# Level 6 of a chunked RWKV-6 attention in quarters of the TensorE array, its masked copies replaced by rectangles

## The chip, the cores and the metric

One core of one Trainium2 chip. The metric is the device time of a whole launch in microseconds (us), lower is better. The kernel before takes 628.2 us, the median of three runs (627.67 to 628.48).

## What is computed

An RWKV-6 attention with a decay for each channel (4 batch rows, 8 heads, 768 steps, head size 48), and behind it a feed-forward block with a SiLU (3072 tokens, 384 to 2048 to 384), all in float32:

```python
for t in range(S):
    cur = np.einsum('bhd,bhe->bhde', u[None] * kt, vt)
    y[:, :, t] = np.einsum('bhd,bhde->bhe', rt, state + cur)
    state = wt[:, :, :, None] * state + np.einsum('bhd,bhe->bhde', kt, vt)
...
x = np.ascontiguousarray(attn_out.transpose(0, 2, 1, 3)).reshape(B * S, H * D)
h = x @ w_in
g = h * (1.0 / (1.0 + np.exp(-h)))
return (g @ w_out).astype(np.float32)
```

## The kernel before, in words

**Units.** The work is cut into 12 units, numbered from 0: 6 chunks of 128 time steps, each for 2 batch rows (b = 0 and 1). In a unit the 8 heads of a batch row are 4 pairs p with two heads e = 0 and 1 each; head e of a pair lies on partitions 64e to 64e + 47 of the transposed tokens. The tokens of batch row 1 are kept in reversed order in places, so that one product serves both rows.

**Levels.** Inside a chunk the recurrence is unrolled by doubling. The scores of a step against an earlier one are found at the level l at which the two fall into the two halves of a block of 2c steps, c = 2^l; levels run from 0 to 6, and at level 6 (c = 64) there is one block: the queries of steps 64 to 127 against the keys of steps 0 to 63. `tr` holds the queries, `tk` the keys and `tw` the products of decays; from level to level, queries (`grow_queries` L604, `prepare` L729) and keys (`grow_keys` L610, `odd_keys` L592) are multiplied by those products.

**Score products.** `score_products` (L661) makes a level's scores with 8 matmuls, one for each pair p and head e. Each takes 48 rows of keys, 128 key columns wide, and moves 128 query columns, 64 of each batch row; the two heads lie on the two row halves of the array and write two PSUM tiles, `sc[0]` and `sc[1]`. So every level computes 128 by 64 scores for each head and batch row, of which the mask of the level keeps a part. `keep_masked` (L676) copies the kept part into the tile `score` with one predicated copy on VectorE (DVE) for each e. For level 6 the mask keeps a plain rectangle for each batch row: 64 rows by 64 columns. `scores` (L682) does products and copies one after the other, and already uses rectangles on ScalarE (ACT) at L698 for the copies listed in COPIED, all of unit 0.

**Bursts.** From unit 2 on (NTOK = 2) levels 3 and 4, and 5 and 6, are made in bursts (`burst`, L743): both levels' products stand one behind the other on TensorE (PE), level 5 in the tile p_sc and level 6 in p_m (in unit 2 in p_o). The copies of a burst follow in `keep_level` (L751), the growing of keys and queries in `go_on` (L755).

**After the scores.** The bonus term (the u of the reference) is written over `score` on its diagonal: in units 2 and 3 by `bonus_spread` (L561, the ACT copies L575 and L577, the DVE shuffle L578) and `bonus_write` (L581, the predicated copies L584), later by `block_spread` and `block_write` (L546 and L553, L557), ahead of the burst of levels 5 and 6. Unit 2 is the one unit from there on whose bonus comes behind that burst. `turn_k` (L773) transposes the keys on PE, which ACT copies to kq (L782). `y_state` (L789, L794) multiplies the state with the queries, `y` (L797, L807) the scores with the values, and `update` (L813, L821) makes the new state; GpSimd (POOL) decays the state at L826, DVE adds to it at L835. `move_x` moves the outcome by DMA to xt.

**Feed-forward.** `up` (L924, L929) multiplies xt with w_in and ACT applies the SiLU from PSUM (L938; two PSUM buffers, p_h). From unit 1 on the second product is done by `quarter` (L981, L995), seven products for eight in the manner of Strassen, whose sums of gt DVE makes at L977; before that `down` (L946, L951).

**Order.** Every engine works through its own queue in the order in which the program was written out, with waits on semaphores; nothing is reordered by a planner. The order is written by hand: units 0 to 2 in a list of `do` calls (L1036 to L1093), the others in `mix` (L867), which gives groups of attention steps, between which L1095 to L1107 put `up` and `quarter` steps of earlier units. In unit 2 the line is

```python
do((burst, 2, 5), (keep_level, 2, 5), (keep_level, 2, 6), (go_on, 2, 6), (up, 1, 6), (bonus_spread, 2), (bonus_write, 2),
   (load_values, 3), *both(turn_k, 2), (up, 1, 7), (sums, 1, 2))
```

and in later units the burst, `keep_level` 5 and 6 and `go_on` 6 are one group, followed by `up` steps.

Of the kernel before, what the change touches and what calls it, by code (L numbers as in the profile page):

```python
# [38 lines left out]
def kernel(  # L39
# [11 lines left out]
    nc = tc.nc  # L51

    B, H, S, D = r.shape
    DM, DF = moe_w_in.shape
    L = 128
    NL = 7
    NB = 2
    NP = H // 2
    PD = 64
    Q = NB * NP  # L60
    NX = Q + 2 * NP
    X = 0, NP + Q
# [5 lines left out]
    NTOK = 2  # L68
# [250 lines left out]
    NSC = 1  # L319
    score = const.tile([128, NSC, 2, Q, L], F32, name="score")  # L320

    masks = {}
    first = {}
    for l in range(NL):
        c, ni = 1 << l, L >> (l + 1)
# [18 lines left out]
    tw, tr, tk, diag, kq, xt = {}, {}, {}, {}, {}, {}  # L344
# [311 lines left out]
        start_keys(i, nc.gpsimd, False)  # L656


    COPIED = (0, 5, 0), (0, 6, 0), (1, 6, 0)

    def score_products(i, l, queries, sc):  # L661
        c, ni = 1 << l, L >> (l + 1)

        for p in range(NP):
            for e in range(2):
                rows = slice(PD * e, PD * e + D)

                apart, r_p, s_p = 2 * (NP - p) - 1, queries[rows, p, :], sc[e][:, p, :]
                nc.tensor.matmul(bass.AP(tensor=s_p.tensor, offset=s_p.offset,  # L669
                                         ap=[s_p.ap[0], [apart * L // 2, 2], [1, L // 2]]),  # L670
                                 lhsT=tk[i][rows, X[l % 2] + p, :],
                                 rhs=bass.AP(tensor=r_p.tensor, offset=r_p.offset + c,
                                             ap=[r_p.ap[0], [apart * L, 2], [2 * c, ni], [1, c]]),
                                 start=True, stop=True)

    def keep_masked(i, l, e, sc):  # L676
        c, ni = 1 << l, L >> (l + 1)
        dst = score[:, i % NSC, e].rearrange("p (b q) (i s c) -> p b q i s c", b=NB, s=2, c=c)[:, :, :, :, 1, :]
        nc.vector.copy_predicated(out=dst, mask=masks[l][:, :, None].to_broadcast([128, NB, NP, ni, c]),  # L679
                                  data=sc[e].rearrange("p (b q) (i c) -> p b q i c", b=NB, c=c))  # L680

    def scores(i, l, *between):  # L682
        c, ni = 1 << l, L >> (l + 1)

        name = "p_h" if i == 0 and l % 2 == 1 else "p_sc"
        sc = [ps.tile([128, Q, L // 2], F32, name=name, bufs=2) for e in range(2)]
        score_products(i, l, tr[i], sc)
        if i < NTOK and l + 2 < NL:
            odd_keys(i, l + 1)

        def keep(e):
            if (i, l, e) in COPIED:

                for b in range(NB):
                    for x in range(ni):
                        first = 2 * x * c if b == 0 else L - (2 * x + 1) * c
                        rows, columns = slice(first, first + c), slice((2 * x + 1) * c, (2 * x + 2) * c)
                        nc.scalar.copy(out=score[rows, i % NSC, e, b * NP:(b + 1) * NP, columns],  # L698
                                       in_=sc[e][rows, b * NP:(b + 1) * NP, x * c:(x + 1) * c])
                return  # L700
            keep_masked(i, l, e, sc)
# [39 lines left out]
    made = {}  # L741

    def burst(i, l):  # L743

        other = (second[0], "p_o") if i == NTOK else (ps, "p_m")
        for x, (pool, name) in enumerate(((ps, "p_sc"), other)):
            made[i, l + x] = [pool.tile([128, Q, L // 2], F32, name=name, bufs=2) for e in range(2)]
        score_products(i, l, before.pop((i, l)), made[i, l])
        score_products(i, l + 1, tr[i], made[i, l + 1])

    def keep_level(i, l):  # L751
        for e in range(2):
            keep_masked(i, l, e, made[i, l])

    def go_on(i, l):  # L755

# [110 lines left out]
    def mix(i):  # L867
# [22 lines left out]
        if i < NPAIR:  # L890
            groups = [[*both(turn, i, "w"), (product, i, 0)],
                      [*both(turn, i, "k"), *both(turn, i, "r"), (odd_ones, i)], [(start_levels, i), (prepare_keys, i, 1)],
                      [(prepare, i, 1), *[(product, i, l) for l in range(1, NL)]],
                      [(burst, i, 1), (keep_level, i, 1)],
                      [(keep_level, i, 2), (go_on, i, 2)],
                      [(prepare, i, 3), (reverse_v, i), (bonus, i, 0)],
                      [(burst, i, 3), (keep_level, i, 3), (bonus_sum, i, 0), (bonus, i, 1), (bonus, i, 2)],
                      [(keep_level, i, 4), (go_on, i, 4), (bonus_sum, i, 1), (load_rk, i + 1), (load_u,)],
                      [(prepare, i, 5), (make_block_mask,), (bonus_spread, i), (bonus_write, i)],
                      [(burst, i, 5), (keep_level, i, 5), (keep_level, i, 6), (go_on, i, 6)], *end]  # L900
        else:
            groups = [[], [(odd_keys, i, 2), (grow_keys, i, 2, False), (grow_queries, i, 2), *sum_steps(i, 2)],
                      [(prepare, i, 3), *bonus_steps(i, 6, 7)],
                      [(burst, i, 3), (keep_level, i, 3), *sum_steps(i, 3, 4), (block_move, i), *at(ahead, (load_rk, i + 1))],
                      [(keep_level, i, 4), (go_on, i, 4)],
                      [(prepare, i, 5), (reverse_v, i)],
                      [(block_spread, i), (block_write, i)],
                      [(burst, i, 5), (keep_level, i, 5), (keep_level, i, 6), (go_on, i, 6)], *end]
# [231 lines left out]
```

## Time and profile before

| | |
|---|---|
| median of 3 runs | 628.2 us (627.67 to 628.48) |
| the profiled execution's own time | 628.39 us |
| its span | 626.6 us |
| PE busy | 620.3 us (99%) |
| DVE busy | 438.6 us (70%) |
| POOL busy | 363.7 us (58%) |
| ACT busy | 187.4 us (30%) |
| granted TensorE clock | 1.00 |

The profile is one execution of the program. Times are in us from the start of its span, unless marked ns. A line of a group or of the timeline names the kernel's line, the engine, the operation, the tile written and the tiles read, the shapes, and how many instructions are taken together. PE is the matmul and PEld the load of its weights, which overlaps other matmuls; every float32 matmul of the program leaves two records of each. The length of a matmul record is longer than the distance to the next one, since matmuls are pipelined: what a matmul costs is read from start to start. The chain of work is followed back from the last instruction to what released each step.

### The profile page before, as it was taken

The page shows a single profiled execution, that of the slowest core. Times are in us where ns is not written, and L with a number is a line of the kernel's source. Part 1 is how long each engine was busy: PE and PEld are TensorE (multiplying, and loading weights), DVE is VectorE, ACT ScalarE, POOL GpSimd, SP SyncE. Part 2 cuts the span into 40 slices and gives each one's busy share as a digit, 9 for nine tenths or more (in the row PEclk, how much of TensorE's full clock was granted, in tenths as well). Part 3 has the DMA queues.
Part 4 walks back from the last instruction along what each step waited for, and adds up shares of the span by engine and source line. Part 5 has one row for each costly group of instructions (what it writes and reads, how often), then busy time and mean ns, then how long its engine had stood idle before and what let it go on. Part 6 is the DMA issues. An engine that isn't in the chain of part 4 may idle for free.

```text
span 626.6 us, 12324 instructions
## 1 busy us (share of the span) xinstructions
PE 620.3 (99%) x4606; PEld 562.8 (90%) x4606; DVE 438.6 (70%) x749; ACT 187.4 (30%) x380; POOL 363.7 (58%) x414
## 2 busy tenths in 40 slices
PE   8999999999999999999999999999999999999997
PEld 8888876799899899899899899889889989989997
DVE  6879779898995694794794595686596596571041
ACT  6798882221321320320320321221221221220110
POOL 6998388566676567567577378378378458400000
PEclk9999999999999999999999999999999999999999
DMA  9966874443543643543543543542542312100000
GB/s 227 291 154 163 164 203 49 88 79 66 101 68 50 133 66 68 106 69 63 105 67 54 110 65 52 115 64 51 115 70 50 77 33 51 35 1 27 25 1 25
DMA packets 203067, 53.25 MB, mean 85 GB/s; under 512 B 186752, under 2 KB 194816, under 8 KB 203008
## 3 DMA queue, kind: packets, MB, share of 16 engines
q1 hardware_dynamic: 201424, 51.88, 41.1%
q10 hardware_dynamic: 1584, 0.59, 0.4%
q8 instruction: 36, 0.59, 0.4%
q14 instruction: 23, 0.19, 0.1%
HBM read 43.21 MB, written 5.24 MB: 77 GB/s over the span
## 4 chain that ended last, share of the span: by engine, by line
PE 94%; POOL 1%; DVE 1%; ACT 1%; DMA 1%; issue 1%; POOLq 0%; ACTq 0%
PE p_h L929 41%; PE p_o L995 32%; PE p_sc L669 5%; PE p_m L951 3%; PE p_m L807 3%; PE p_m L794 3%; PE p_m L669 3%; PE p_m L781 1%; PE p_sc L821 1%; DMA raw<-in_k_dram 1%; PE p_m L372 1%; POOL tk L625 1%; PE p_m L845 0%; DVE score L584 0%; POOL w_in_sb L241 0%
## 5 line engine op out<-in xcount | busy, mean ns | idle before, releaser
L929 PE MATMUL p_h<-xt,w_in_sb 128*128 128x256 f32 x1152 | 258.1, 382 | 0.7 <-POOL tk L649 0.7
L929 PEld LDWEIGHTS p_h<-xt,w_in_sb 128*128 128x128 f32 x1152 | 215.9, 190 | 32.6 <-POOL tk L649 0.9
L938 ACT ACTIVATE gt<-p_h 128x512 f32<-128x512 f32 x90 | 53.7, 597 | 256.1 <-PE p_h L929 255.9
L625 POOL TENSOR_TENSOR tk<-tk,tw 128x256 f32<-128x256 f32 x128 | 88.7, 714 | 62.4 <-ACT tk L595 34.7
L995 PE MATMUL p_o<-own,temps 128*128 128x192 f32 x528 | 87.9, 326 | 0.0
L995 PE MATMUL p_o<-w_out_sb,gt 128*128 128x192 f32 x508 | 87.3, 328 | 0.0
L995 PEld LDWEIGHTS p_o<-own,temps 128*128 128x128 f32 x528 | 86.0, 190 | 0.2
L995 PEld LDWEIGHTS p_o<-w_out_sb,gt 128*128 128x128 f32 x508 | 82.7, 190 | 0.9 <-issue 0.4
L487 POOL TENSOR_TENSOR ruk<-tokens_rk 128x768 f32<-128x768 f32 (+1 forms) x32 | 48.5, 1527 | 46.3 <-DMA tokens_rk<-in_k_dram 33.7
L977 DVE TENSOR_TENSOR temps<-gt 128x256 f32<-128x256 f32 x84 | 55.4, 660 | 18.3 <-ACT gt L938 18.3
L408 POOL TENSOR_TENSOR tw<-tw 128x256 f32<-128x256 f32 (+6 forms) x83 | 43.8, 528 | 40.2 <-DVE tw L360 36.3
L679 DVE COPY_PREDICATED score<-mask,p_sc 128x512 f32<-128x512 int8 x62 | 44.5, 772 | 13.4 <-PE p_sc L669 12.7
L607 DVE TENSOR_TENSOR tr<-tr,tw 128x512 f32<-128x512 f32 x61 | 49.6, 813 | 3.7 <-POOL tk L625 1.1
L595 ACT COPY tk<-tk 128x256 f32<-128x256 f32 x52 | 20.9, 403 | 85.4 <-POOL tk L625 67.1
L1004 DVE TENSOR_TENSOR partial<-p_o,partial 128x192 f32<-128x192 f32 x33 | 11.8, 358 | 47.2 <-PE p_o L995 47.1
L669 PEld LDWEIGHTS p_sc<-tr,tk 48*128 48x128 f32 x512 | 31.4, 187 | 10.3 <-issue 7.3
L669 PE MATMUL p_sc<-tr,tk 48*128 48x128 f32 x512 | 37.7, 285 | 0.7 <-POOL tk L625 0.6
L1004 DVE TENSOR_TENSOR temps<-p_o,partial 128x192 f32<-128x192 f32 x22 | 7.9, 358 | 33.3 <-PE p_o L995 23.1
L995 PE MATMUL p_o<-w_out_sb,temps 128*128 128x192 f32 x176 | 30.4, 326 | 0.0
L995 PEld LDWEIGHTS p_o<-w_out_sb,temps 128*128 128x128 f32 x176 | 28.9, 190 | 0.0
L487 POOL TENSOR_TENSOR tokens_rk<-tokens_rk,tokens_w 128x192 f32<-128x192 f32 (+1 forms) x32 | 26.8, 857 | 1.3
L977 DVE TENSOR_TENSOR temps<-temps,gt 128x256 f32<-128x256 f32 x43 | 25.7, 598 | 1.5
(170 smaller groups left out, 828.0 us busy)
## 6 DMA issues: line engine op xcount, KB each, us to landing
w_out_sb<-in_moe_w_in_dram SPq DMA_DIRECT2D x6, 768.0 KB, 7.0
w_out_sb<-in_moe_w_out_dram SPq DMA_DIRECT2D x4, 768.0 KB, 5.1
own<-in_moe_w_out_dram SPq DMA_DIRECT2D x4, 768.0 KB, 5.1
tokens_rk<-in_r_dram SPq DMA_DIRECT2D x8, 384.0 KB, 4.5
tokens_rk<-in_k_dram SPq DMA_DIRECT2D x8, 384.0 KB, 5.3
tokens_w<-in_w_dram SPq DMA_DIRECT2D x8, 384.0 KB, 6.6
xt<-yt SPq DMA_DIRECT2D x60, 48.0 KB, 2.0
raw<-in_w_dram SPq DMA_DIRECT2D x80, 32.0 KB, 2.3
```

What stands on the lines that cost most here:

```text
L408: engine.tensor_tensor(out=up, in0=t[:, :, 0::2], in1=t[:, :, 1::2], op=ALU.mult)
L487: mul = lambda out, one, two: nc.gpsimd.tensor_tensor(out=out, in0=one, in1=two, op=ALU.mult)
L595: nc.scalar.copy(out=keys(i, X[(l + 1) % 2] * L + c, [4 * c, blocks], [c, 2], [1, c]), in_=keys(i, NP * L + c, [4 * c, blocks], [NP * L + ...
L607: nc.vector.tensor_tensor(out=odd, in0=odd, in1=tw[i][l][:, :, 0::2][:, :, :, None].to_broadcast([128, Q, L >> (l + 1), c]), op=ALU.mult)
L625: nc.gpsimd.tensor_tensor(out=out, in0=have, in1=odd_products(i, l, b, *blocks), op=ALU.mult)
L669: nc.tensor.matmul(bass.AP(tensor=s_p.tensor, offset=s_p.offset, ap=[s_p.ap[0], [apart * L // 2, 2], [1, L // 2]]), lhsT=tk[i][rows, X[l % ...
L679: nc.vector.copy_predicated(out=dst, mask=masks[l][:, :, None].to_broadcast([128, NB, NP, ni, c]), data=sc[e].rearrange("p (b q) (i c) -> ...
L929: nc.tensor.matmul(p_h[:, a, :], lhsT=w_in_sb[:, c, f * 128:(f + 1) * 128], rhs=xt[i][:, c, :], start=(c == 0), stop=(c == KC - 1))
L938: nc.scalar.activation(out=gt[i, m], in_=p_h, func=AF.Silu)
L977: nc.vector.tensor_tensor(out=out, in0=one, in1=two, op=op)
L995: nc.tensor.matmul(p, lhsT=left(f), rhs=right[:, f, :], start=(f == 0), stop=(f == FH - 1))
L1004: nc.vector.tensor_tensor(out=to, in0=p, in1=known, op=ALU.add)
```

## The change

Levels from APART = 6 on, in units from 2 on, are computed in another way. For each pair p, each of the two key halves x and each head e there is one matmul: 48 rows by 64 key columns against the 64 query columns of one batch row alone (x = 0 with batch row 0, x = 1 with batch row 1). It lies on rows 64e and columns 64x of the array, and writes partitions 64x to 64x + 63 of `sc[e]`. So 16 matmuls stand where 8 stood; the half of the old products that the mask threw away is not computed. The order is p, then x, then e. `keep_level` copies two rectangles of 64 partitions by 256 elements for each e in place of one predicated copy: those of e = 0 on DVE, those of e = 1 on ACT. On ACT they stand in the queue where `keep_level` stands; the first waits for the matmuls of `sc[1]` and for DVE's level-5 copy of e = 1. Nothing is moved in the written order, and no DMA is added.

```diff
+    APART = 6
+
+    def corner(l, x):
+
+        return x % 2, x if x % 2 == 0 else (L >> l) - 1 - x
+
...
     def score_products(i, l, queries, sc):
         c, ni = 1 << l, L >> (l + 1)
+        if i >= NTOK and l >= APART:
+            for p in range(NP):
+                for x in range(L // c):
+                    b, first = corner(l, x)
+                    q = (p, 2 * NP - 1 - p)[b]
+                    for e in range(2):
+                        rows = slice(PD * e, PD * e + D)
+                        nc.tensor.matmul(sc[e][x * c:(x + 1) * c, q, first // 2 * c:(first // 2 + 1) * c],
+                                         lhsT=tk[i][rows, X[l % 2] + p, x * c:(x + 1) * c],
+                                         rhs=queries[rows, q, (first + 1) * c:(first + 2) * c], start=True, stop=True)
+            return
...
     def keep_level(i, l):
+        c = 1 << l
         for e in range(2):
-            keep_masked(i, l, e, made[i, l])
+            if l < APART:
+                keep_masked(i, l, e, made[i, l])
+                continue
+            for x in range(L // c):
+                b, first = corner(l, x)
+                (nc.vector.tensor_copy if e == 0 else nc.scalar.copy)(
+                    out=score[x * c:(x + 1) * c, i % NSC, e, b * NP:(b + 1) * NP, (first + 1) * c:(first + 2) * c],
+                    in_=made[i, l][e][x * c:(x + 1) * c, b * NP:(b + 1) * NP, first // 2 * c:(first // 2 + 1) * c])
```

In the changed kernel the lines below the edit have moved: the quarter matmuls are L676 and the old form of the products L686, the rectangles L776, the SiLU L963, the state's product with the queries L819, the scores' product with the values L832.

## Prediction

> **What bounds the kernel now.** I read the busy shares first, then the chain of work that ended last, then the timeline of one steady unit, and last the timeline of unit 2, the first one that the change touches (units count from 0; the "third unit" is unit 2).
>
> From the page, busy shares and the chain by engine:
>
> ```profile
> PE 620.3 (99%) x4606; PEld 562.8 (90%) x4606; DVE 438.6 (70%) x749; ACT 187.4 (30%) x380; POOL 363.7 (58%) x414
> ...
> PE 94%; POOL 1%; DVE 1%; ACT 1%; DMA 1%; issue 1%; POOLq 0%; ACTq 0%
> ```
>
> TensorE is busy 620.3 of 626.6 us and makes 94% of the chain. So a nanosecond taken from its queue is a nanosecond of the end, as long as nothing else becomes late; DVE, ACT and POOL time counts only where TensorE has to wait for it.
>
> The timeline of unit 10 around the burst that the change edits (start, length, engine, line):
>
> ```profile
> 505.23 1.16 PE L669 MATMUL p_sc<-tr,tk 48*128 48x128 f32 x16
> 506.22 1.06 PE L669 MATMUL p_m<-tr,tk 48*128 48x128 f32 x16
> 506.42 1.34 DVE L679 COPY_PREDICATED score<-mask,p_sc 128x512 f32<-128x512 int8 x2
> 507.21 8.04 PE L929 MATMUL p_h<-xt,w_in_sb 128*128 128x256 f32 x36
> 507.65 1.33 DVE L679 COPY_PREDICATED score<-mask,p_m 128x512 f32<-128x512 int8 x2
> 516.96 1.08 PE L807 MATMUL p_m<-score,vt 128*48 128x128 f32 x16
> ```
>
> Level 5 writes p_sc and level 6 p_m, 16 records each: every f32 matmul leaves two records. Level 6 takes 506.22 to 507.21. Its copies end near 509.0 and their reader, L807, comes at 516.96: 8 us of cover, filled by "up" matmuls.
>
> **What the Trainium skill says.** (1) "TensorEngine Tiling (Array Packing)", Key Properties: separate tiles of the array load and multiply in parallel, but a change of tiling mode drains TensorE. The trace agrees: in single records, the two heads of a pair start 6 to 7 ns apart, and the last full-array "up" record is 309 to 310 ns from the first half-array record, where it is 215 from another full one: 94 ns for the drain. (2) "TensorE: Matmul & The Clock Gate", Part 3, the measured speedups: row and column tiles compose, at about 4 ns of issue per tile. No matmul of this trace is tiled both ways, so four at once is unshown here. (3) "SBUF — State Buffer", SBUF: two separate sides: a VectorE instruction with two SBUF inputs and a GpSimd one lock each other out for whole instructions. The trace agrees: L557 takes 1.3 us, but 2.9 where it started just after a GpSimd instruction.
>
> **The change, part by part.** *The matmuls.* Removed in each of the ten units 2 to 11: 8 matmuls (16 records) of level 6, moving 128 columns on half the array, two at a time. Their pairs start 111.6 ns apart, so 8 pairs take 893 ns. Added: 16 matmuls (32 records), 64 columns wide, 64 columns moving, on a quarter each. The slot of a quarter is read between two rows. A pair of L821 (48 by 48) takes 45 ns, from these lines of unit 2, 0.36 us for 16 records:
>
> ```profile
> 127.42 0.53 PE L821 MATMUL p_sc<-vt,kq 128*48 128x48 f32 x16
> 127.78 0.53 PE L821 MATMUL p_sc<-vq,kq 128*48 128x48 f32 x16
> ```
>
> From 48 to 128 columns the slot grows by 66.6 ns, or 0.83 a column, so 64 columns take 45 + 16 x 0.83 = 58 ns. If four quarters run at once, 32 records are 8 slots: 466 ns.
>
> *The change of mode.* Before, levels 5 and 6 shared one mode. Now there is a switch between them: 94 ns of drain, and a first weight load that nothing hides. That load shows as a longer first slot after a switch: 213 instead of 112 ns at 128 weight columns (L669), 80 instead of 45 at 48 (L821). For 64 I take 50. So 144 ns are added; the switch back to the full array was there before. I bound the entry by 0 (a quarter may count as the same row mode) and 200 (the full L669 price).
>
> Sum per unit: 893 - (144 + 466) = 283 ns saved. Over the nine units 3 to 11: 2.5 us.
>
> *The copies.* Two predicated copies of 128x512 (715 ns each on DVE) become two of 64x256 on DVE and two on ACT. ACT has that very shape in L698, 367 ns from PSUM, so ACT gains 0.73 us a unit. For DVE I take 0.42 us (L955 takes 549 ns for 384 elements; 128 fewer at about 1 ns), so DVE loses about 0.6 us a unit. In units 3 to 11 I cost both at nothing: the cover is the 8 us above (10 us in unit 3). The first ACT copy waits for DVE's second level-5 copy, because both write head 1's part of `score`, and the SiLUs queue behind it. In unit 10 that ends at 507.76, the copies would end near 508.6, and the next SiLU is due at 510.10. Hidden.
>
> *Unit 2 has no such cover.* DVE is late there, and the bonus still has to be written after the scores:
>
> ```profile
> 119.52 1.32 DVE L679 COPY_PREDICATED score<-mask,p_sc 128x512 f32<-128x512 int8 x2
> 120.74 1.33 DVE L679 COPY_PREDICATED score<-mask,p_o 128x512 f32<-128x512 int8 x2
> ...
> 122.77 2.50 DVE L584 COPY_PREDICATED score<-own_mask,both_b 128x1024 f32<-128x1024 int8 x2
> ```
> ```profile
> 120.49 0.60 ACT L938 ACTIVATE gt<-p_h 128x512 f32<-128x512 f32 x1 [7.16 <-PE p_h L929]
> 120.99 0.20 ACT L575 COPY both_b<-diag 128x16 f32<-128x16 f32 x1
> 121.55 0.84 ACT L577 COPY both_b<-diag 32x16 f32<-32x16 f32 x4 [0.37 <-DMA diag<-own_sums]
> ```
> ```profile
> 123.76 1.95 PE L794 MATMUL p_m<-tr,state 128*128 128x128 f32 x16
> 125.64 1.08 PE L807 MATMUL p_m<-score,vt 128*48 128x128 f32 x16
> ```
>
> The chain is ACT L577, then DVE's shuffle L578 and bonus write L584 (ending 125.27), then TensorE's L807 at 125.64; so there are under 0.4 us to spare. The ACT copies now stand ahead of the SiLU at 120.49, and they wait until 120.84 for DVE. So: copies to 121.64, SiLU to 122.25, L575 and four L577 (0.2 and 0.84 us) to 123.2, where it was 122.39. The shuffle and L584's 2.50 us end at 126.1, and L807 starts near 126.15 instead of 125.64: 0.5 us lost instead of 0.28 won. DVE and POOL carry their lateness into unit 3, where POOL's level-2 keys (136.72 + 2.81 = 139.53) were only 0.2 us ahead of the matmuls that need them at 139.74; I add 0.15. Unit 2 costs 0.65 us, with bounds of 0 to 0.8.
>
> Total: 2.5 - 0.65 = 1.9 us. The profiled execution took 628.39 us (span 626.6 and 1.8 around it), so it becomes 626.5; the median of the three runs, 628.2, lies 0.2 below it. Forecast: 626.3.
>
> **The rivals.** *Locked out in unit 2* (627.5): POOL's state update L826 follows the first half of L794 and starts about 0.1 us after DVE's second bonus write in my sum. Were it to come first, that write (mask and data both in SBUF) waits for the whole of L826, 1.24 us, and L807 with it: 626.3 + 1.24. For it: the margin is small, and L557 shows the price. Against: both hang on the same ACT work, so the margin moves little.
>
> *No loss in unit 2* (625.4): ten units at 283 ns. It needs the ACT copies to run clear of DVE's lateness; the wait on DVE's second level-5 copy speaks against it.
>
> *Limited by issue* (628.6): if no more records get through than L821 shows, 22.5 ns each, 32 take 720 ns; with 144 that leaves 29 ns, 0.26 us in nine units, less than unit 2's 0.65. For it: that rate is the fastest in the trace. Against: there it is set by 48 columns, not by issue; within a pair records start 7 ns apart.
>
> *Two at a time* (630.5, slower): if quarters overlap only in pairs, 32 records are 16 slots, 933 ns; with the switch 1,077, which is 184 more than before. Nine units: 1.65, and 0.65 for unit 2. It decides from 23.4 ns a record up ((893 - 144) / 32). Against it: row pairs (L669) and column pairs (L807, L821) both overlap fully. For it: their combination is nowhere in the trace.
>
> **How the numbers follow.** Forecast 0.45, locked out 0.19, two at a time 0.14, no loss 0.13, issue 0.09. A measurement can tell about 0.2%, 1.26 us, from no change: faster ends at 626.9, slower begins at 629.5. Faster: most of the forecast (0.41), no loss (0.13) and a little of the lock case: 0.56. Same: 0.28. Slower: 0.16. The range runs from 625.2 (no loss, with a cheaper switch) to 628.7 (issue) and leaves out two at a time and the tails.
>
> **What would show it.** In the profile after: the quarters (L676) start 58 ns apart in fours, and level 6 takes 0.7 us from its first record to the next "up", where it took 0.99. Their count is 32 a unit. From unit 3 on each unit is 0.28 us shorter and L832 (the former L807) shows no wait; in unit 2 it waits for DVE's L584 and starts near 126.1. ACT's L776 takes 0.37 us. I am wrong on the step of four at once if level 6 takes as long as before or longer, on the switch if the first quarter follows level 5 within 112 ns, and on unit 2 if L832 there follows the state matmuls (L819) at once.

## The result and the profile after

The changed kernel takes 627.09 us, the median of 16 runs (626.6 to 628.11), where the kernel before takes 628.24 in the same series (16 runs, 627.67 to 629.39). The ratio is 0.9979, with a 95% interval of 0.9972 to 0.9987: 0.8 to 1.8 us less, 1.15 in the middle. The forecast was 626.3, so the gain has the sign and the order that I gave it, and 0.8 us of it is missing. The medians are 0.18% apart, a little under the 0.2% from which I called a kernel faster; the interval, 0.13 to 0.28%, does not reach zero.

The profiled execution of the changed kernel took 626.69 us, with a span of 624.8 (before: 628.39 and 626.6). From its page, busy shares and the chain by engine:

```profile
PE 617.9 (99%) x4766; PEld 558.8 (89%) x4766; DVE 437.0 (70%) x749; ACT 194.6 (31%) x400; POOL 365.1 (58%) x414
...
PE 91%; DVE 3%; POOL 2%; ACT 1%; DMA 1%; issue 1%; SPq 0%; POOLq 0%; DVEq 0%; ACTq 0%
```

TensorE has 160 records more (ten units, 16 each) and is busy 2.4 us less. But its share of the chain has gone from 94 to 91%, and DVE's from 1 to 3%: the first sign that something else has become late.

The timeline of unit 10 around the burst, the same stretch as before:

```profile
503.97 1.16 PE L686 MATMUL p_sc<-tr,tk 48*128 48x128 f32 x16
505.07 0.69 PE L676 MATMUL p_m<-tr,tk 48*64 48x64 f32 x32
505.17 1.35 DVE L696 COPY_PREDICATED score<-mask,p_sc 128x512 f32<-128x512 int8 x2
505.69 4.15 PE L954 MATMUL p_h<-xt,w_in_sb 128*128 128x256 f32 x18
506.41 0.84 DVE L776 COPY score<-p_m 64x256 f32<-64x256 f32 x2
506.61 0.75 ACT L776 COPY score<-p_m 64x256 f32<-64x256 f32 x2 [1.93 <-DVE score L696]
```

From the first record of level 5 to the next "up" it is 1.72 us, where it was 1.98. Level 6 itself takes 0.62 us where it took 0.99; it begins 1.09 us after level 5 where it began 0.99 after it, since there is now a switch between the two. In single records: 208 ns from the last pair of level 5 to the first quarter (112 without a switch, so 96 to 97 for the drain), 107 for the first slot (49 more than a full slot), then slots of four quarters 58.3 ns apart, whose members start 7 ns apart. From the last slot to the next "up" it is 168 ns, which is 110 more than a slot; before it was 208, 96 more than a slot. Together 0.269 us less per unit, in all ten units alike.

The timeline of unit 2, by engine, VectorE first:

```profile
118.99 1.33 DVE L696 COPY_PREDICATED score<-mask,p_sc 128x512 f32<-128x512 int8 x2
120.21 0.84 DVE L776 COPY score<-p_o 64x256 f32<-64x256 f32 x2
...
122.76 0.01 DVE L578 LOAD_MASK_SELECT both_b<-both_b  x1 [0.98 <-ACT both_b L577]
...
122.96 2.50 DVE L584 COPY_PREDICATED score<-own_mask,both_b 128x1024 f32<-128x1024 int8 x2
```
```profile
120.41 0.75 ACT L776 COPY score<-p_o 64x256 f32<-64x256 f32 x2 [7.61 <-DVE score L696]
121.17 0.60 ACT L963 ACTIVATE gt<-p_h 128x512 f32<-128x512 f32 x1
121.67 0.20 ACT L575 COPY both_b<-diag 128x16 f32<-128x16 f32 x1
121.87 0.84 ACT L577 COPY both_b<-diag 32x16 f32<-32x16 f32 x4
122.62 1.05 ACT L807 COPY kq<-p_m 128x512 f32<-128x512 f32 x2
```
```profile
123.25 2.05 PE L819 MATMUL p_m<-tr,state 128*128 128x128 f32 x16
125.23 1.25 PE L832 MATMUL p_m<-score,vt 128*48 128x128 f32 x15
...
127.09 0.30 PE L846 MATMUL p_sc<-vt,kq 128*48 128x48 f32 x3
127.19 0.27 PE L832 MATMUL p_m<-score,vq 128*48 128x128 f32 x1
```

It is the chain of the forecast: the ACT copies wait for DVE's second level-5 copy, the SiLU and the bonus copies queue behind them, VectorE idles 0.98 us for L577, and TensorE waits for L584 in the middle of L832.

**The unit by unit account.** I lay the records of TensorE of both profiles side by side and take the difference of their times. One thing has to be taken off first: by the end of unit 1, which the change doesn't touch, this profile is already 0.53 us ahead of that of before. That is scatter of the launches (the leads of the experiments' profiles at that place lie between 0.78 ahead and 0.23 behind), and no gain. "Quarter products" are those of `quarter` in the feed-forward part (L1020); they have nothing to do with the quarters of the array. Past that lead, in us:

| | forecast | the change | e1 | e3 | e4 |
|---|---|---|---|---|---|
| level 6, in each unit that has it | -0.283 | -0.269 | none | -0.269 | -0.269 |
| its units, summed | -2.55 (units 3 to 11) | -2.69 (2 to 11) | 0 | -2.42 (3 to 11) | -2.69 |
| lost in unit 2 (forecast: net of its level 6) | 0.50 | 0.67 | 0.39 | 0 | 0 |
| lost at the level-2 keys of unit 3 | 0.15 | 0.26 | 0.26 | 0 | 0.06 |
| lost in the quarter products of unit 3 | 0 | 0.37 | -0.05 | 0.48 | 0.54 |
| lost in the quarter products of unit 4 | 0 | 0.13 | 0.16 | 0.37 | 0.26 |
| sum | -1.90 | -1.26 | 0.76 | -1.57 | -1.83 |

(e1 to e4 are experiments, below.) Each column is one execution; the medians give -1.15, 0.41, -1.90 and -2.26 for the last four sums, so the account is good to about 0.4 us. From unit 5 on nothing is lost. The two rows that the forecast has at 0 are what was not foreseen. The page of the changed kernel names them in the group of the quarter products' weight loads:

```profile
L1020 PEld LDWEIGHTS p_o<-own,temps 128*128 128x128 f32 x528 | 86.0, 190 | 0.7 <-DVE temps L1029 0.6
```

Before, that group had 0.2 us of idle time and no releaser was named. L1029 (L1004 before) is the addition on VectorE that empties a p_o buffer. In unit 3 of the kernel before:

```profile
186.05 0.54 DVE L521 TENSOR_REDUCE block_sums<-spare 128x8 f32<-128x384 f32 x1
186.62 0.36 DVE L1004 TENSOR_TENSOR temps<-p_o,partial 128x192 f32<-128x192 f32 x1
187.28 0.36 DVE L1004 TENSOR_TENSOR partial<-p_o,partial 128x192 f32<-128x192 f32 x1 [0.31 <-PE p_o L995]
```

And in unit 3 of the changed kernel:

```profile
167.17 0.69 DVE L607 TENSOR_TENSOR tr<-tr,tw 128x512 f32<-128x512 f32 x1
167.89 1.93 DVE L1002 TENSOR_TENSOR temps<-gt 128x256 f32<-128x256 f32 x1
169.85 1.10 DVE L1002 TENSOR_TENSOR temps<-temps,gt 128x256 f32<-128x256 f32 x1
170.88 1.24 DVE L1002 TENSOR_TENSOR temps<-gt 128x256 f32<-128x256 f32 x1
172.04 0.41 DVE L1002 TENSOR_TENSOR temps<-gt,temps 128x256 f32<-128x256 f32 x1
...
186.28 0.54 DVE L521 TENSOR_REDUCE block_sums<-spare 128x8 f32<-128x384 f32 x1
186.85 0.36 DVE L1029 TENSOR_TENSOR temps<-p_o,partial 128x192 f32<-128x192 f32 x1
```
```profile
165.27 1.82 POOL L487 TENSOR_TENSOR ruk<-tokens_rk 128x768 f32<-128x768 f32 x1 [5.04 <-DVE score L584]
...
170.75 1.08 POOL L487 TENSOR_TENSOR tokens_rk<-tokens_rk,tokens_w 128x384 f32<-128x384 f32 x1
```

One and the same VectorE instruction, L1002, takes 0.41 us alone and 1.93, 1.10 and 1.24 while GpSimd's L487 run, and each of these three ends about 0.28 us behind the end of one L487 (the lock that the Trainium skill, "SBUF — State Buffer", SBUF: two separate sides, describes). (The bracket of the first L487 names L584, which ended about when the load of tokens_rk landed; in the kernel before and in e12 it names that load.) From there to 187.2 VectorE has no gap that a bracket would show: it goes from lock to L1029 at full load. So L1029 comes when the lock and the work behind it are over, not when TensorE is ready for it, and TensorE waits there 0.47 us from one record to the next (then 0.27), where a step is 0.16. In the kernel before one step at that place took 0.21: TensorE was already 0.05 us early there. At the start of unit 3 the engines still stand alike, 0.13 us later than before on the profile's clock (VectorE's L696 at 150.16, L679 before at 150.03). Then TensorE wins 0.27 at level 6, and VectorE loses 0.1: its L1029 begins at 186.85, 0.23 later than before. The two together are the 0.37 of the table. In unit 3 the margin for the gain was nil.

### The profile page after: what moved, and what is told of

Same layout as the page of the kernel before. It is cut to its first block, busy times and chain, and to the rows that moved or that the text cites. A ratio compares the mean times of both kernels' runs of the same rounds, so it can differ in the third digit from the quotient of the medians.

```text
span 624.8 us, 12663 instructions
## 1 busy us (share of the span) xinstructions
PE 617.9 (99%) x4766; PEld 558.8 (89%) x4766; DVE 437.0 (70%) x749; ACT 194.6 (31%) x400; POOL 365.1 (58%) x414
## 4 chain that ended last, share of the span: by engine, by line
PE 91%; DVE 3%; POOL 2%; ACT 1%; DMA 1%; issue 1%; SPq 0%; POOLq 0%; DVEq 0%; ACTq 0%
PE p_h L954 40%; PE p_o L1020 32%; PE p_sc L686 5%; PE p_m L832 3%; PE p_m L819 3%; PE p_m L976 3%; PE p_m L686 1%; POOL tk L625 1%; DMA u_bc<-in_u_dram 1%; PE p_m L806 1%; PE p_sc L846 1%; PE p_m L676 1%; PE p_m L870 0%; DVE score L584 0%; SPq L93 0%
## 5 line engine op out<-in xcount | busy, mean ns | idle before, releaser
L963 ACT ACTIVATE gt<-p_h 128x512 f32<-128x512 f32 x90 | 53.6, 597 | 217.3 <-PE p_h L954 217.1
L1020 PE MATMUL p_o<-own,temps 128*128 128x192 f32 x528 | 88.3, 327 | 0.1
L1020 PE MATMUL p_o<-w_out_sb,gt 128*128 128x192 f32 x508 | 87.4, 328 | 0.0
L1020 PEld LDWEIGHTS p_o<-own,temps 128*128 128x128 f32 x528 | 86.0, 190 | 0.7 <-DVE temps L1029 0.6
L1020 PEld LDWEIGHTS p_o<-w_out_sb,gt 128*128 128x128 f32 x508 | 82.7, 190 | 0.9 <-issue 0.4
L487 POOL TENSOR_TENSOR ruk<-tokens_rk 128x768 f32<-128x768 f32 (+1 forms) x32 | 50.6, 1590 | 45.7 <-DMA tokens_rk<-in_k_dram 24.2
L1002 DVE TENSOR_TENSOR temps<-gt 128x256 f32<-128x256 f32 x84 | 54.5, 649 | 18.4 <-ACT gt L963 18.3
L696 DVE COPY_PREDICATED score<-mask,p_sc 128x512 f32<-128x512 int8 x62 | 44.6, 772 | 14.9 <-PE p_sc L686 14.3
L607 DVE TENSOR_TENSOR tr<-tr,tw 128x512 f32<-128x512 f32 x61 | 51.0, 837 | 4.0 <-POOL tk L625 1.1
L1029 DVE TENSOR_TENSOR partial<-p_o,partial 128x192 f32<-128x192 f32 x33 | 11.8, 358 | 45.0 <-PE p_o L1020 44.9
L686 PEld LDWEIGHTS p_sc<-tr,tk 48*128 48x128 f32 x512 | 31.4, 187 | 10.3 <-issue 6.7
L686 PE MATMUL p_sc<-tr,tk 48*128 48x128 f32 x512 | 37.7, 285 | 0.7 <-POOL tk L625 0.7
L1029 DVE TENSOR_TENSOR temps<-p_o,partial 128x192 f32<-128x192 f32 x22 | 7.9, 358 | 33.2 <-PE p_o L1020 22.9
L1020 PE MATMUL p_o<-w_out_sb,temps 128*128 128x192 f32 x176 | 30.4, 326 | 0.0
L1020 PEld LDWEIGHTS p_o<-w_out_sb,temps 128*128 128x128 f32 x176 | 28.9, 190 | 0.0
L1002 DVE TENSOR_TENSOR temps<-temps,gt 128x256 f32<-128x256 f32 x43 | 26.7, 622 | 1.5
L487 POOL TENSOR_TENSOR tokens_rk<-tokens_rk,tokens_w 128x192 f32<-128x192 f32 (+1 forms) x32 | 26.6, 851 | 1.3
```

The source lines that it names most:

```text
L487: mul = lambda out, one, two: nc.gpsimd.tensor_tensor(out=out, in0=one, in1=two, op=ALU.mult)
L607: nc.vector.tensor_tensor(out=odd, in0=odd, in1=tw[i][l][:, :, 0::2][:, :, :, None].to_broadcast([128, Q, L >> (l + 1), c]), op=ALU.mult)
L963: nc.scalar.activation(out=gt[i, m], in_=p_h, func=AF.Silu)
L1002: nc.vector.tensor_tensor(out=out, in0=one, in1=two, op=op)
L1020: nc.tensor.matmul(p, lhsT=left(f), rhs=right[:, f, :], start=(f == 0), stop=(f == FH - 1))
L1029: nc.vector.tensor_tensor(out=to, in0=p, in1=known, op=ALU.add)
```

## The experiments

My theory after the result: three things make the time. (A) The quarters win 0.27 us a unit. (B) In unit 2 and at the keys of unit 3 the ACT copies give 0.66 us back. (C) In units 3 and 4 TensorE, quicker by level 6, runs into VectorE at L1029 and gives 0.50 us back. The main rivals are that unit 2 is late for another reason, that (C) is only unit 2's lateness handed on, and that four quarters do not run at once but the gain comes from somewhere else. All medians are beside runs of the kernel before on the same chip (628.2 to 628.3).

### e1: the copies alone

```diff
-        if i >= NTOK and l >= APART:
+        if False:
```

> Old level-6 products on the half array in every unit, but the copies as rectangles on VectorE and ScalarE: the copies alone. Theory (the copies make unit 2 late, and what follows it): nothing is won on TensorE; unit 2 loses about 0.4 us at the scores' product with the values, the level-2 keys of unit 3 another 0.25, later units nothing; about 628.9 us, slower than before by 0.6. Rival (the copies cost nothing, TensorE only runs ahead into VectorE once the quarters make it faster): the same as before, 628.2.

Measured: 628.63 us (628.19 to 630.05), ratio 1.0010 [1.0002, 1.0018]. The rectangles by themselves make the kernel 0.1 to 1.1 us slower. In the trace the loss stands where it was expected, 0.39 in unit 2 and 0.26 at the level-2 keys. It also has 0.16 in the quarter products of unit 4, where nothing was expected and no quarter makes TensorE earlier; GpSimd's L487 start 0.35 us later there than before (213.75 for 213.40).

### e3: the whole change, but only from unit 3 on

```diff
-        if i >= NTOK and l >= APART:
+        if i > NTOK and l >= APART:
...
-            if l < APART:
+            if l < APART or i == NTOK:
```

> The whole change from unit 3 on, unit 2 as before. Theory (the copies in unit 2 start the loss): nine units win 0.27 us each, no wait in unit 2 nor at the level-2 keys of unit 3, and little in the quarter products of units 3 and 4: 2.2 to 2.4 us less than before, about 625.9. Rival (TensorE runs into a VectorE that has no slack in units 3 and 4, whatever unit 2 does): the 0.5 us of waits in those quarter products stays, and the time is about 626.4.

Measured: 626.32 us (625.62 to 627.02), ratio 0.9971 [0.9960, 0.9983]. Nothing is lost in unit 2 and at the keys, so (B) is shown from both sides. But the quarter products now lose 0.48 and 0.37, though unit 2 hands on no lateness. Of the 0.48, 0.27 is the win of unit 3 itself; the rest is VectorE, which comes to L1029 later within the unit, as GpSimd's first L487 does (165.58, 165.14 before). The rival's number (626.4) came out, not that of the theory with (B) alone (625.9).

### e4: unit 2's ACT rectangles behind the bonus

```diff
-    do((burst, 2, 5), (keep_level, 2, 5), (keep_level, 2, 6), (go_on, 2, 6), (up, 1, 6), (bonus_spread, 2), (bonus_write, 2),
-       (load_values, 3), *both(turn_k, 2), (up, 1, 7), (sums, 1, 2))
+    do((burst, 2, 5), (keep_level, 2, 5), (keep_level, 2, 6, [0]), (go_on, 2, 6), (up, 1, 6), (bonus_spread, 2),
+       *both(turn_k, 2), (keep_level, 2, 6, [1]), (bonus_write, 2), (load_values, 3), (up, 1, 7), (sums, 1, 2))
```

> The whole change, but in unit 2 the two ScalarE rectangles stand behind the bonus copies and the two key copies of ScalarE, and the bonus write on VectorE behind them. Theory: the chain from the bonus copies to the bonus write keeps its old times, the scores' product with the values waits no longer, ten units win 0.27 us each: about 625.6 to 625.9, 2.3 to 2.7 us less than before. Rival (VectorE's lateness in unit 2 comes from elsewhere): unit 2 still loses 0.4 us and the time stays at 627.

Measured: 625.96 us (625.45 to 626.15), ratio 0.9962 [0.9949, 0.9974], better than the change. From the timeline of TensorE in unit 2, L832 now stands behind L819 without a wait and without a stray record:

```profile
122.90 1.95 PE L819 MATMUL p_m<-tr,state 128*128 128x128 f32 x16
124.78 1.08 PE L832 MATMUL p_m<-score,vt 128*48 128x128 f32 x16
125.69 1.04 PE L832 MATMUL p_m<-score,vq 128*48 128x128 f32 x16
```

Unit 2 keeps its 0.27, and the keys lose 0.06. So what cost unit 2 was the place of two ACT copies in ACT's queue, not their work. 0.80 us still goes at L1029.

### e5: the same quarters in an order that allows pairs only

```diff
-            for p in range(NP):
-                for x in range(L // c):
+            for x in range(L // c):
+                for p in range(NP):
```

> The change with the loop over the key halves outside: all eight matmuls of one column half first, then those of the other, so that only the two row tiles can overlap. Theory (four quarters at once give the win): 16 slots of 58 ns in place of 8, 0.466 us more a unit on TensorE, of which unit 2 and the waits of units 3 and 4 swallow about 0.9: about 631 us, slower than before. Rival (the order is of no matter): 627.1, as the change itself.

Measured: 629.36 us (628.41 to 629.98), ratio 1.0015 [1.0008, 1.0021]: slower than before. Unit 10 in its timeline:

```profile
507.68 0.98 PE L676 MATMUL p_m<-tr,tk 48*64 48x64 f32 x32
508.58 1.13 PE L954 MATMUL p_h<-xt,w_in_sb 128*128 128x256 f32 x4
```

Level 6 takes 0.91 us, not 0.62. So the gain of the change is indeed the overlap of both column halves (A). The size was off: I reckoned with 16 slots, the records show 13, because three slots in the middle hold four records: the second column half begins before the first has ended. Level 6 is still 0.08 us shorter than before, but the switches eat that up, and the loss of the copies (e1) remains.

### e7 and e8: VectorE's sums moved away from L1029

VectorE's sums L521 of the next unit, which stand just ahead of L1029, and GpSimd's bonus steps that follow them go from the end of a unit to the next one, behind its first three quarter products; e7 does it to e4, e8 to the kernel before.

```diff
-               [*both(y_state, i), *both(y, i), *both(update, i), *at(ahead, *start(i + 1)),
-                *at(ahead, *sum_steps(i + 1, 0, 1), *bonus_steps(i + 1, 4, 5)), (move_x, i)]]
+               [*both(y_state, i), *both(y, i), *both(update, i), *at(ahead, *start(i + 1)), (move_x, i)]]
...
-            groups = [[], [(odd_keys, i, 2), (grow_keys, i, 2, False), (grow_queries, i, 2), *sum_steps(i, 2)],
+            groups = [[], [*sum_steps(i, 0, 1), *bonus_steps(i, 4, 5), (odd_keys, i, 2), (grow_keys, i, 2, False), (grow_queries, i, 2), *sum_steps(i, 2)],
```

> The kernel e4 (the change with unit 2's ScalarE rectangles put behind the bonus) with one move more: VectorE's block sums 0 and 1 (L521's form) and GpSimd's bonus steps 4 and 5 (L487) of the next unit stand no longer at the end of a unit but in the next one, behind its first three quarter products, from unit 3's end on. Theory: the 0.8 us that TensorE loses in the quarter products of units 3 and 4 come from VectorE being late at the addition that frees p_o, behind those sums; with them out of the way the waits there go and the median falls by 0.6 to 0.8 us against e4, to 625.2 to 625.4 us. Rival: VectorE leaves the stretch of the mutual lock with GpSimd at the same time whatever stands in it, or the moved sums are late at their new place; then it stays at 625.7 to 626.2, or the waits come back under another line.

> The kernel before with the same move of VectorE's block sums and GpSimd's bonus steps alone, nothing of the change. Theory (in the kernel before VectorE is only just in time at that place, TensorE waits 0.2 us there at most): 628.0 to 628.4 us, no difference that can be measured. Rival (the move helps by itself, through less locking between VectorE and GpSimd): 627.4 or less.

Measured: e7 627.71 us (627.39 to 628.06), ratio 0.9992 [0.9984, 1.0001]; e8 630.29 us (630.13 to 631.38), ratio 1.0037 [1.0024, 1.0050]. Both expectations missed: the move costs 2 us by itself. In e8's trace TensorE loses 0.30 us in every unit from 3 on, at a quarter product about 5 us behind L1029's place, where VectorE now comes late. The rival of e7 (the wait comes back elsewhere) has it. Still the pair shows (C) for unit 3. There, with e7's edit, L1029 (in e7 L1028) begins earlier and has idle time behind it, in which it waits for TensorE and not TensorE for it:

```profile
185.49 0.36 DVE L1028 TENSOR_TENSOR temps<-p_o,partial 128x192 f32<-128x192 f32 x1
186.39 0.36 DVE L1028 TENSOR_TENSOR partial<-p_o,partial 128x192 f32<-128x192 f32 x1 [0.55 <-PE p_o L1019]
```

In unit 4 the move does not help: L1028 begins at 234.89, in e4 L1029 at 234.82, and TensorE still waits 0.44 us; GpSimd's L487 start later there (214.87, in e4 213.19). In that unit e7 is spared the 0.30 us that e8 loses further on. So from e8 to e7 the quarters bring nearly all of their 2.7 us: the median falls by 2.58.

### e12: all four rectangles on VectorE

```diff
-                (nc.vector.tensor_copy if e == 0 else nc.scalar.copy)(
+                nc.vector.tensor_copy(
```

> The change with all four rectangles on VectorE, none on ScalarE: VectorE gets 0.83 us more in each of ten units, ScalarE's bonus copies in unit 2 are where they were before. Theory (in units 3 and 4 VectorE leaves the stretch that it shares with GpSimd when GpSimd does, whatever copies it had to make before): unit 2 keeps about 0.2 us more than in the change, the waits in the quarter products of units 3 and 4 stay at 0.4 to 0.8 us together, 626.0 to 626.7 us. Rival (VectorE's copies count one for one there): 0.8 us more of waiting in unit 3 and 0.8 in unit 4, 627.5 to 628.5.

Measured: 627.49 us (626.33 to 627.83), ratio 0.9984 [0.9975, 0.9993]; between the two expectations. Unit 2 keeps 0.18 us more than in the change. VectorE has 0.83 us more to do in unit 3 (and as much in unit 2), but it comes to L1029 only 0.30 us later, at 187.15. This alone does not show that the copies do not count: VectorE's bonus write L584 began 0.59 us earlier than in the change (162.10 for 162.69, its DMA landed earlier), so that VectorE came to the sums only 0.30 later as well. And GpSimd's first L487 started 0.29 later, at 165.56, behind a DMA issue L139 that took 1.27 us for 0.62. What shows the lock is a comparison over the runs, in unit 3:

| | VectorE's L607, ahead of the sums L1002 | end of GpSimd's last L487 | VectorE's L360, behind the sums | between the last two |
|---|---|---|---|---|
| before | 166.05 | 172.28 | 173.61 | 1.33 |
| the change | 167.17 | 171.84 | 173.84 | 2.00 |
| e4 | 166.00 | 171.05 | 173.05 | 2.00 |
| e8 | 165.49 | 170.81 | 172.81 | 2.00 |
| e12 | 167.47 | 172.14 | 174.14 | 2.00 |

VectorE leaves the stretch 2.00 us behind GpSimd, whenever it came; e7, e9, e11 and e13 give 2.00 too. (In the kernel before, as in e1, two sums, 0.34 us from start to start, got through in a pause that GpSimd made for a DMA, 0.95 us long before; in e3 it was one, and 1.66.) The wait grew by 0.65 us, because TensorE came 0.35 earlier and VectorE 0.30 later. My number for it (0.4 to 0.8 in all) was too small: it was 1.02 in unit 3, and none in unit 4.

### e14: GpSimd's load earlier

If the lock in unit 3 is due to the start of L487, an earlier load of its data should undo it.

```diff
-                      [(keep_level, i, 4), (go_on, i, 4), (bonus_sum, i, 1), (load_rk, i + 1), (load_u,)],
+                      [(keep_level, i, 4), (go_on, i, 4), (load_rk, i + 1), (load_u,), (bonus_sum, i, 1)],
```

> The change with one thing more: in unit 3 the loads of tokens_rk, tokens_w and u_bc for unit 4 are issued ahead of the four small diag loads and not behind them (SyncE's queue, 154 us instead of 159). Theory (VectorE is late at L1029 in unit 3 because GpSimd's four bonus instructions L487 start when that load lands, at 165.3 us, and stretch VectorE's instructions until 172): GpSimd starts near 161, VectorE reaches L1029 0.5 us or more earlier, the wait of 0.4 us in unit 3's quarter products goes, unit 4's stays; 626.6 to 626.8 us. Rival (GpSimd then locks VectorE's bonus write L584 and VectorE is as late as before, or later): the wait stays or grows, 627.1 us or more.

Measured: 628.67 us (628.17 to 629.60), ratio 1.0007 [0.9999, 1.0015], the gain of the change gone. GpSimd starts at 160.08, and the L1002 that took 1.93 us takes 0.43. VectorE is through the sums L521 ahead of L1029 at 186.51, but that is only 0.31 us earlier than in the change, not 0.5. The wait in unit 3's quarter products goes, yet TensorE comes there 2.1 us later than in the change, so it would have gone without the earlier sums. The lock has moved to other work, and this makes TensorE late. The timelines of VectorE, ACT and TensorE in unit 3:

```profile
164.08 3.81 DVE L584 COPY_PREDICATED score<-own_mask,both_b 128x1024 f32<-128x1024 int8 x2
...
170.59 0.43 DVE L1002 TENSOR_TENSOR temps<-gt 128x256 f32<-128x256 f32 x1
```
```profile
169.19 0.74 ACT L776 COPY score<-p_m 64x256 f32<-64x256 f32 x2 [4.39 <-DVE score L696]
169.96 1.08 ACT L963 ACTIVATE gt<-p_h 128x512 f32<-128x512 f32 x2
```
```profile
164.38 5.45 PE L954 MATMUL p_h<-xt,w_in_sb 128*128 128x256 f32 x24 [1.20 <-ACT gt L963]
170.61 1.56 PE L954 MATMUL p_h<-xt,w_in_sb 128*128 128x256 f32 x6 [0.78 <-ACT gt L963]
```

The bonus write L584 takes 3.81 us for 2.50 and also starts later (its diag loads now stand behind the big ones), DVE's level-5 copies follow it, the ACT rectangle waits 4.39 us for the second of them, and the SiLU behind it comes so late that TensorE waits 0.78 us. (The 1.20 ahead of it come from the late bonus copies on ACT, which hold up the SiLU before.) So the ACT rectangles that the forecast called "hidden" in later units have a margin too: here they came 2.7 us later than in the change, which the cover did not bear. Of the theory the going of that wait came true, of the rival the lock on L584 and the time; so this run does not settle what the load's landing is worth in the change.

### e9, e11 and e13: level 5 in quarters too

The account points to a better version: the switch is paid once for two levels, if level 5 is in quarters too. For level 5 a quarter takes 64 keys against 32 queries of each batch row, 64 columns again; its mask stays, with four predicated copies of 64x256 for two of 128x512. From unit 3 on:

```diff
+    def halved(i, l):
+        return i >= NTOK + 1 and 5 <= l < NL - 1
...
+                        nc.tensor.matmul(bass.AP(tensor=s_p.tensor, offset=s_p.offset + x * half // 2,
+                                                 ap=[s_p.ap[0], [apart * half + (1 - 2 * x) * half // 2, 2], [1, half // 2]]),
+                                         lhsT=tk[i][rows, X[l % 2] + p, x * half:(x + 1) * half],
+                                         rhs=bass.AP(tensor=r_p.tensor, offset=r_p.offset + c + x * half,
+                                                     ap=[r_p.ap[0], [apart * L + (1 - 2 * x) * half, 2], [2 * c, ni // 2], [1, c]]),
+                                         start=True, stop=True)
```

e9 is e7 with it, e11 is e4 with it, and e13 is e11 with the move of e7 in the units 3 and 4 alone.

> e7 with level 5 too in quarters of the array from unit 3 on: 16 matmuls, 48 rows by 64 key columns against 32 query columns of each batch row, and four predicated copies of 64 partitions in place of two of 128. By the prediction's own terms: level 5 takes 8 slots of 58 ns (466) instead of 893, the switch of 144 ns between the levels goes, the entry gets about 50 ns cheaper, so some 0.6 us a unit on TensorE, 5.4 us in nine units: 620 us if nothing becomes late. Against it VectorE gets four copies of about 0.45 us for two of 0.72, some 0.4 us a unit more; if that is what TensorE then waits for, the gain is 1.5 to 3 us only, 622.5 to 624.

> e9 without the move of VectorE's sums: e4 with level 5 in quarters from unit 3 on. In e9 TensorE still waited 0.3 us in each of units 5 to 11 for the moved sums, and not before L1029. Theory (TensorE's gains stand except where VectorE is late in units 3 and 4): it loses up to 0.9 and 0.7 us there again and wins 0.3 in each of seven or eight later units, so 621.0 to 622.2 us. Rival (the four predicated copies make VectorE late at L1029 in every unit): 623.5 to 625.

> e11 with VectorE's sums and GpSimd's bonus steps moved in units 3 and 4 alone, where VectorE is late at L1029 (the addition of the quarter products that frees p_o). Theory: e9's 0.3 us in each of units 5 to 11 goes, and of e11's 1.1 and 2.1 us of waiting in units 3 and 4 at most 0.2 and 1.1 stay: 620.5 to 621.8 us. Rival (what e9 lost in the later units comes from the halves' four copies and not from the moved sums): about 623.2 us as e9.

Measured: e9 623.25 us (622.62 to 623.91), ratio 0.9921 [0.9907, 0.9934]; e11 624.67 (621.80 to 625.82), ratio 0.9934 [0.9917, 0.9950]; e13 **621.44** (621.19 to 621.90), ratio 0.9887 [0.9872, 0.9902]. e13 beats both kernels, by 6.9 us and by 5.7. Unit 10 of e13, TensorE:

```profile
500.52 0.69 PE L685 MATMUL p_sc<-tr,tk 48*64 48x64 f32 x32
501.04 0.65 PE L680 MATMUL p_m<-tr,tk 48*64 48x64 f32 x32
501.61 2.21 PE L983 MATMUL p_h<-xt,w_in_sb 128*128 128x256 f32 x9
```

Both levels take 1.09 us, against 1.72 in the change and 1.98 before: the 0.6 us a unit that the terms of the forecast give. e9 came into the second of its ranges, but not because of the four copies: its 0.3 us in each later unit go in e13, which has the same copies. e11 missed its number. It came into the range of its rival, but not by the rival's cause: its waits are not in every unit. It is the clearest case of (C). Its page has

```profile
L1049 PE MATMUL p_o<-own,temps 128*128 128x192 f32 x528 | 90.1, 331 | 3.2 <-DVE temps L1058 3.2
```

3.2 us of waiting at this one place, in units 3 and 4, where up to 1.6 was expected. In unit 4 VectorE idles 7 us for the bonus, which comes by way of a DMA (of `spare`), and is late from there on; the loads for GpSimd's L487 stand behind that DMA in the queue, and L487 starts at 215.74, in the change at 213.83. And the longer of the two waits costs more than itself. The busy time by stretch in unit 4 (columns: stretch, its length, busy us and instructions of TensorE, its weight loads, VectorE, ACT and GpSimd, then the granted clock of TensorE, the share of the DMA engines and GB/s):

```profile
235.00:237.70 2.70, 0.69 (x5) 0.40 (x3) 2.66 (x6) 0.41 (x1) 1.21 (x2) 1.00 0.23 62
...
238.70:242.30 3.60, 3.60 (x14) 3.60 (x13) 1.13 (x4) 0.00 (x0) 3.52 (x6) 0.53 0.28 57
242.30:246.00 3.70, 3.70 (x25) 3.70 (x24) 1.38 (x4) 0.93 (x2) 3.62 (x5) 1.00 0.41 50
```

After 2.42 us from one record to the next, TensorE is granted about half its clock for 3.6 us, its records come 0.32 us apart and not 0.16, and another 1.6 us are lost. Three of e11's six runs show a mean clock of 0.997 and take 625.3 to 625.8 us, the other three show 1.00 and take 621.8 to 624.1: this is a good part of e11's spread. In e13 one wait of 1.1 us is left, in unit 4, with no loss of clock behind it, and the 0.3 us of e9's later units are gone, as expected.

## Why the prediction was right, and where not

**Right, with its number.** Four quarters run at once: slots of 58.3 ns for the forecast 58, and e5 shows that the overlap of the column halves is what pays. That row and column tiles compose, which the Trainium skill, "TensorE: Matmul & The Clock Gate", Part 3, states and no trace of before had, is thereby measured here. The change of mode costs 97 and 49 ns for the forecast 94 and 50, and the sum per unit is 269 ns for 283. Most of the 14 ns between them is the switch back to the full array, which I took as unchanged: it costs 13 ns more than before. ACT's rectangle takes 367 ns as read from L698, VectorE's 414 for the estimated 420.

**Right in its sum.** Unit 2 with the keys cost 0.66 us net of its level 6 (0.67 + 0.26 - 0.27), forecast 0.65. That the two agree to 0.01 us is luck: unit 2 net of its level 6 cost 0.40 for the forecast 0.5, the keys 0.26 for 0.15. The chain on ACT and DVE holds to about 0.1 us once the lead of 0.53 is added: L584 ends at 125.46, or 125.99 on the clock of before, forecast 126.1. But two steps behind it went another way. L832 did not start near 126.1 but at 125.23: its first part (head e = 0) needs only the first bonus write, and the wait fell on the second. And one wait was not foreseen at all: the copies of kq (L807 in the changed kernel), which stand in ACT's queue behind the bonus copies, hold up L819 by 0.28 us. I had named the queue behind the waiting copy as far as L577, and stopped one step short.

**Wrong: "In units 3 to 11 I cost both at nothing", with "as long as nothing else becomes late".** In the change the copies themselves were hidden from unit 3 on; but I had looked for lateness only at what the change moves. What became late for the quicker TensorE is VectorE's L1029 in units 3 and 4, which the change doesn't touch: 0.37 + 0.13 us of the 2.7 were lost there, 0.80 in e4, 0.85 in e3, and in e11, with level 5 in quarters, TensorE idles 3.2 us there. With 9 times 14 ns for the smaller win per unit this makes up the 0.6 us between the forecast sum (1.90) and the traced one (1.26). The median's 0.8 holds 0.1 to 0.2 us of scatter besides. The trace of before showed the place: L1004 began there at 186.62 directly after VectorE's sums, and one step of the quarter products at that place took 0.21 us in place of 0.16. I read the cover of the copies and did not ask which wait TensorE meets when it comes earlier.

**Rivals.** The median, 627.09, lies nearer to "locked out in unit 2" (627.5) than to the forecast, and the range was wide enough to take in no change at all, so the number by itself proves little. The trace excludes that rival: L584 took its 2.50 us as before, and GpSimd's state update was the one that got longer (3.02 us for 2.42). It excludes "no loss in unit 2" and "limited by issue" too. Two at a time is excluded for the change, and e5, with its 13 slots, shows a part of its price: 0.28 us a unit more than the change, where I had put 0.47 for 16. A lock did decide something, but of L1002 by L487, one unit later.

**Open.** Why the profiles differ by up to 1 us before the change begins was not looked into, nor why the load and the bonus DMA ahead of L1029 land up to 1 us earlier or later from run to run. That VectorE leaves the lock in unit 3 with GpSimd is shown by the five runs of the table; no run shows what the gain would be with the load alone earlier. In unit 4, where the load, the bonus DMA and VectorE's own queue all come into it, nothing was taken away one by one, and e1 loses as much there (0.16) as the change (0.13).

## What to carry to other kernels

When a bound engine gets quicker, look in the trace of before for the places where it was only just not waiting, a step that is 50 ns too long or a releaser that ends with no idle time of its own; each of them can cap the gain, and removing the next part of the work is then worth less until that releaser moves (e4 saves 0.87 us in unit 2 and at the keys, and loses 0.30 of it at L1029). A copy that is off the critical path is free by its work but not by its place: in an in-order queue it hands its own wait to all that stands behind it, and here moving two copies behind the urgent ones was worth 1.1 us, nearly 0.2%. A switch of the array's mode was paid here each time, about 0.15 us with its first slot, so it pays to put what uses the new mode side by side, as e13 does.

## What the runs showed of the hardware that I had not expected

- Matmuls on different column tiles do not keep strictly to the order of the program: in unit 2 three records of L846 start at 127.09, ahead of the last L832 at 127.19 that stands before them; in e5 the second column half begins three slots before the first ends.
- When VectorE comes to a stretch in which GpSimd locks it out changes its exit from that stretch little: it came to it at times from 165.49 (e8) to 167.47 (e12), and was through with the sums there 2.00 us behind the end of GpSimd's last L487 in both.
- TensorE's clock falls after a shorter wait than I had thought: 2.42 us between two records in e11 were followed by 3.6 us at a granted clock of 0.53, 1.4 us in e9 and e13 by no loss of clock. The Trainium skill, "TensorE: Matmul & The Clock Gate", Part 1, has an idle window of about 3.4 us for that; here less was enough once.
- An earlier load can be a loss: in e14 GpSimd's start 5 us earlier moved the lock from the sums (1.93 us for 0.43) to the bonus write (3.81 us for 2.50), which has more behind it.
